# The spare-item loop of an attention + MoE + SwiGLU kernel: one chunk of both matrices per turn of an inner loop

## The chip, the cores and the metric

One core of a Trainium2 chip runs the whole program in one launch. The metric is the device time of one execution in microseconds (us). Engines are named as in the profile: PE is TensorE (its weight loads are PEld, its sequencer PEq or PEldq), DVE is VectorE, ACT is ScalarE, POOL is GpSimd, SP is SyncE, which here only issues transfers.

## What is computed

Three stages in a row, on 1536 tokens of 512 values, all in float32:

```python
x = attention(q, k, v)            # 8 heads, a band of 16 keys each way + 24 block summaries
logits = x @ w_gate + modality_bias[modality_id]
e_idx = argmax(logits); gate_w = softmax(logits)[e_idx]
for e in range(8):                # each token goes to one expert
    h = relu(x[e_idx == e] @ w1[e])            # 512 -> 1024
    y[e_idx == e] = gate_w * (h @ w2[e])       # 1024 -> 512
out = (silu(y @ w_g) * (y @ w_v)) @ w_o        # 512 -> 1536 -> 512
```

## The kernel before

The program has a written-out order on every engine. The attention comes first, the routing is computed beside its end, then the experts follow (the MoE), and then the dense SwiGLU stage.

**The experts.** Every product of two float32 matrices is made of three PE products of a high and a low part (`mm3`, L805 to L808). The tokens of an expert are gathered into items. Five items stand in the program as straight code (`KIND = "TQQSP"`): the largest expert takes an item of three blocks of 128 tokens, then come two of four blocks, one of a single block and one of two blocks. Each item multiplies by `w1` in four chunks of 256 hidden columns (`hidden`) and by `w2` (`project`). Its weight chunks, 512 KB each, are fetched by SP (L802), so the five items make 5 x 8 = 40 fetches; ACT and DVE split each into a high and a low part (L787, L788).

**The spare loop.** How many items are really needed is known only on the chip. Line 1342 loads the number of items beyond the five, `n_over`, into a register of every engine. At L1363 each engine compares it with zero. If it is positive, the loop at L1364 makes one spare item of two blocks per turn: gather, `split_x` (8 transposes on PE, L767), four `hidden` of 24 products each, and four chunks of `project`, 24 products each. If it is zero, a short else part raises the semaphores by what the body would have added, and jumps over the body (L1363 in the profile as well). The body lies in line in each engine's program, between that jump and the SwiGLU stage.

**Just before the branch** the last item ends: PE's last products of L806 to L808 into `ps_V`, ACT's `yh` (L1357) and DVE's `yl` (L1358), the high and low part of the MoE's output.

**Just behind it** the SwiGLU stage begins (`gv`): PE makes 12 products into `ps_T` for the gate (`gh`, `gl`), 12 for the value (`vh`, `vl`), and so on; ACT loads the table for Silu and makes `sg` (L1403), DVE `hv` (L1405). `ps_T` has three PSUM banks. From there to the end PE works through six blocks of 256 inner columns, while DVE decodes the next block's weights, fetched by SP (L1209). The last block adds each result to `acc` (L1422), and POOL scatters the rows to the output (L1427).

Of the kernel before, what the change touches and what calls it, by code (L numbers as in the profile page):

```python
# [7 lines left out]
F32 = mybir.dt.float32  # L8
F32R = mybir.dt.float32r
# [3 lines left out]
ALU = mybir.AluOpType  # L13
# [6 lines left out]
def sparse_attention_moe_swiglu_kernel(  # L20
# [18 lines left out]
    nc = tc.nc  # L39
    B, H, S, D = q.shape  # L40
# [25 lines left out]
    IT = 256  # L66
# [13 lines left out]
    KD = DM // 128  # L80
    NC1 = FF // 256
# [9 lines left out]
    def bank(tag):  # L91
        t = ps.tile([128, 512], F32, tag=tag, bufs=BANKS[tag], name="ps_" + tag)
        return t
# [81 lines left out]
    ident = const.tile([128, 128], F32, name="ident")  # L175
# [56 lines left out]
    for n in range(6):  # L232
        t = b_p[n // 3].tile([W, NG, H, D + 1], F32, tag=f"ve{n}", name=f"ve{n}")
# [497 lines left out]
    pl = {}  # L731
# [12 lines left out]
    def gather(pool, *cols, rows=NTOK):  # L744
        xs = []
        for ia in cols:
            t = pool.tile([128, DM + 1], F32, tag="xs", bufs=4, name="xs")
            nc.gpsimd.indirect_dma_start(out=t, out_offset=None, in_=x_d[0:rows, :],
                                         in_offset=bass.IndirectOffsetOnAxis(ap=ia, axis=0))
            xs.append(t)  # L750
        return xs

    def scale_x(xs):
        for t in xs:
            nc.vector.tensor_scalar(out=t[:, 0:DM], in0=t[:, 0:DM], scalar1=t[:, DM:DM + 1], scalar2=None, op0=ALU.mult)
# [27 lines left out]
    def split_w(pool, src, eng, tags=("wh", "wl")):  # L783
        a, b = src.shape[1], src.shape[2]
        wh = pool.tile([128, a, b], F32R, tag=tags[0], name="wh")
        wl = pool.tile([128, a, b], F32R, tag=tags[1], name="wl")
        nc.scalar.activation(out=wh, in_=src, func=ACTF.Copy)  # L787
        eng.tensor_tensor(out=wl, in0=src, in1=wh.bitcast(F32), op=ALU.subtract)  # L788
        return wh, wl

    def load_w(pool, e, which, c):
        r = pool.tile([128, KD, 256], F32, tag="raw", name="raw")
        if which == "w1":
            src = w1[bass.ds(e, 1), :, 256 * c:256 * c + 256]
        elif which == "rows":

            src = w2[bass.ds(e, 1), 256 * c:256 * c + 256, :].rearrange("e (k p) f -> p (e k) f", p=128)
            nc.sync.dma_start(out=r.rearrange("p (k a) f -> p k (a f)", k=2), in_=src)
            return r
        else:  # L800
            src = w2[bass.ds(e, 1), 512 * (c % 2):512 * (c % 2) + 512, 256 * (c // 2):256 * (c // 2) + 256]
        nc.sync.dma_start(out=r, in_=src.rearrange("e (k p) f -> p (e k) f", p=128))  # L802
        return r

    def mm3(out_, ah, al, bh, bl, start, stop):  # L805
        nc.tensor.matmul(out=out_, lhsT=ah, rhs=bh, start=start, stop=False)  # L806
        nc.tensor.matmul(out=out_, lhsT=ah, rhs=bl, start=False, stop=False)  # L807
        nc.tensor.matmul(out=out_, lhsT=al, rhs=bh, start=False, stop=stop)  # L808

    def hidden(c, x, w, later=None, tags="TT", between=None):  # L810
        n = x[0].shape[2]
        hh = pl["h"].tile([128, 2, n], F32R, tag="hh", name="hh")
        hl = pl["h"].tile([128, 2, n], F32R, tag="hl", name="hl")
        per = 512 // n
        for f0 in range(0, 2, per):
            if f0 and between is not None:
                between()
            p = bank(tags[f0])[:, 0:per * n].rearrange("p (f c) -> p f c", f=per)
            for f in range(f0, f0 + per):
                sl = slice(128 * f, 128 * f + 128)  # L820
                for kk in range(KD):
                    mm3(p[:, f - f0, :], w[0][:, kk, sl], w[1][:, kk, sl], x[0][:, kk, :], x[1][:, kk, :], kk == 0,
                        kk == KD - 1)
            fs = slice(f0, f0 + per)
            nc.scalar.activation(out=hh[:, fs], in_=p, func=ACTF.Relu)

            def low(p=p, fs=fs):
                nc.vector.scalar_tensor_tensor(out=hl[:, fs], in0=p, scalar=0.0, in1=hh[:, fs].bitcast(F32),  # L828
                                               op0=ALU.max, op1=ALU.subtract)

            if later is None:
                low()
            else:
                later.append(low)
        return hh, hl


    def project(c, hs, w, yp, cols=(0, 1), between=None):
        for k in range(4):
            if k == 2 and between is not None:  # L840
                between()
            kk = 4 * (c % 2) + k
            h = hs[kk // 2]
            for dd in cols:
                sl = slice(128 * dd, 128 * dd + 128)
                own = len(yp) == 1 and len(cols) == 2
                y = yp[0][:, dd] if own else yp[dd][:, 0]
                mm3(y, w[0][:, k, sl], w[1][:, k, sl], h[0][:, kk % 2, :], h[1][:, kk % 2, :],
                    kk == 0 and (dd == 0 or not own), kk == 2 * NC1 - 1 and (dd == 1 or not own))

    def y_banks(n, tag):
        if n == 256:
            return [bank(tag).rearrange("p (d c) -> p d c", d=2)]
        return [bank(tag)[:, 0:n].rearrange("p (d c) -> p d c", d=1) for _ in range(2)]

    def store_y(dp, yp, a, v_):
        for i, y in enumerate(yp):
            nd = 2 // len(yp)
            ds = slice(2 * dp + nd * i, 2 * dp + nd * i + nd)
            nc.scalar.activation(out=yh[:, ds, a], in_=y, func=ACTF.Copy)  # L860
            nc.vector.tensor_tensor(out=yl[:, ds, v_], in0=y, in1=yh[:, ds, v_].bitcast(F32), op=ALU.subtract)
# [141 lines left out]
    for st, names in steps.items():  # L1003
        for nm in names.split():
            b, t, j = (int(c) for c in nm[1:])
# [94 lines left out]
    hs, later = [], []  # L1100
# [19 lines left out]
    yp = [y_banks(CT, "S")]  # L1120
# [146 lines left out]
    def column(j):  # L1267
        return [eng.value_load(tab[0:1, 1, j:j + 1], min_val=0, max_val=before(j)) for eng in (nc.scalar, nc.vector)]
# [6 lines left out]
    hs = []  # L1275
# [5 lines left out]
    sa, sd = column(1)  # L1281
    for c in range(NC1):
        if c % 2 == 0:
            yp = y_banks(512, "T" if c else "S")
# [17 lines left out]
    hs, h1, hb = [], [], []  # L1302
# [19 lines left out]
    sa, sd = column(2)  # L1322
    for c in range(NC1):
        if c % 2 == 0:
            yp = y_banks(512, "T" if c else "S")
# [10 lines left out]
    hs = []  # L1336
# [9 lines left out]
    sa, sd = column(NS - 1)  # L1346
    ws = {}
    for tag, d0, cols in (("S", 0, (0, 1)), ("S", 2, (0,)), ("V", 3, (1,))):
        nd = len(cols)
        yp = bank(tag).rearrange("p (d c) -> p d c", d=2)[:, 0:nd]  # L1350
# [9 lines left out]
    bg_step(100)  # L1360


    with tc.If(n_over > 0, preferred_fallthrough_block=False):  # L1363
        with tc.For_i(0, n_over, 1) as it:  # L1364
            ii = pl["xg"].tile([128, 2], I32, tag="ii", name="ii")
            nc.vector.tensor_copy(out=ii, in_=idx[:, bass.ds(it * NB + NB * NS, 2)])
            e = nc.sync.value_load(tab[0:1, 0, bass.ds(it + NS, 1)], min_val=0, max_val=E - 1)
            xo = gather(pl["xg"], ii[:, 0:1], ii[:, 1:2])
            scale_x(xo)
            xo = split_x(pl["xg"], xo)  # L1370
            hs = [hidden(c, xo, split_w(pl["wc"], load_w(pl["raw"], e, "w1", c), nc.vector)) for c in range(NC1)]
            sa = nc.scalar.value_load(tab[0:1, 1, bass.ds(it + NS, 1)], min_val=0, max_val=NTOK)
            sd = nc.vector.value_load(tab[0:1, 1, bass.ds(it + NS, 1)], min_val=0, max_val=NTOK)
            for c in range(NC1):
                if c % 2 == 0:
                    yp = y_banks(IT, "S")
                project(c, hs, split_w(pl["wc"], load_w(pl["raw"], e, "w2", c), nc.vector), yp)
                if c % 2:
                    store_y(c // 2, yp, bass.ds(sa, IT), bass.ds(sd, IT))
    moe.close()  # L1380


# [94 lines left out]
```

## Time and profile before

| | |
|---|---|
| time, median of 3 runs | 596.92 us (596.2 to 598.31) |
| the profiled execution's own time | 597.52 us |
| its span, first to last instruction | 595.8 us |
| PE busy | 566.1 us, 95% of the span |
| DVE, ACT, POOL busy | 65%, 35%, 12% |
| mean granted clock of PE | 0.985 of full |

What lies around the span is 597.52 - 595.8 = 1.7 us. A time in a row is in us from the span's start. A name that ends in q (PEldq, SPq) is that engine's sequencer: branches, semaphore waits and the issuing of transfers stand there and are not counted as busy. `[4.31 <-issue]` behind a row says that the engine had been idle for 4.31 us before it, and that the profile shows no engine that it waited for. q8 and q14 of kind "instruction" are the queues on which the engines' own programs are fetched.

### The profile page before, as it was taken

Reading aid. Unit: us, or ns where it says so; the run is one execution under the profiler, and the core shown is the slowest. Engines: PE = TensorE matmul, PEld = TensorE weight load, DVE = VectorE, ACT = ScalarE, POOL = GpSimd, SP = SyncE. Lnnn points to the kernel's source line nnn. Section 1 sums busy time; section 2 is a strip of 40 time slices with the busy share of each in tenths; the row PEclk is TensorE's granted clock in tenths of the full one; section 3 lists DMA queues with packets and bytes.
Section 4 is the critical chain, followed back from the end, with each engine's and each line's share of the span. In section 5 each row is a group of like instructions: output and inputs, shape, how many; then the busy total and the mean of one; then the engine's idle time right before and its main releaser. Section 6 shows DMA issues by size and latency. Waiting matters only on the chain.

```text
span 595.8 us, 8863 instructions
## 1 busy us (share of the span) xinstructions
PE 566.1 (95%) x3372; PEld 474.3 (80%) x3372; DVE 384.8 (65%) x760; ACT 211.2 (35%) x370; POOL 69.8 (12%) x196
## 2 busy tenths in 40 slices
PE   7979997998996999999799999999999999999996
PEld 6769985998785888899588888888888888888884
DVE  6667796677978468674257568558738837863323
ACT  6766944443332354363223332212212212211110
POOL 6573012040202000100000000000000000000025
PEclk9999999999997999999899999999999999999999
DMA  9999238445634455561022222112203212200013
GB/s 249 212 261 202 79 91 261 136 146 167 202 127 124 125 174 172 163 202 47 3 72 70 72 80 93 40 36 84 93 0 107 71 36 70 72 0 1 0 72 141
DMA packets 76429, 64.84 MB, mean 109 GB/s; under 512 B 24340, under 2 KB 70432, under 8 KB 76192
## 3 DMA queue, kind: packets, MB, share of 16 engines
q1 hardware_dynamic: 74304, 57.41, 34.8%
q0 software_dynamic: 2080, 6.82, 3.4%
q8 instruction: 28, 0.46, 0.3%
q14 instruction: 17, 0.14, 0.1%
HBM read 57.88 MB, written 6.35 MB: 108 GB/s over the span
## 4 chain that ended last, share of the span: by engine, by line
PE 47%; issue 3%; POOL 2%; DVE 0%; POOLq 0%
PE ps_T L806 11%; PE ps_T L808 11%; PE ps_T L807 11%; PE ps_S L806 2%; PE ps_S L808 2%; PE ps_S L807 2%; POOL out_dram L1427 2%; PE ps_P L806 1%; PE ps_V L806 1%; PE ps_V L808 1%; PE ps_P L807 1%; PE ps_V L807 1%; PE ps_P L808 1%; DVE acc L1422 0%; POOL between L1425 0%
## 5 line engine op out<-in xcount | busy, mean ns | idle before, releaser
L1405 DVE TENSOR_TENSOR hv<-sg,ps_T 128x512 f32<-128x512 f32 x36 | 24.7, 687 | 74.4 <-PE ps_T L808 74.4
L806 PE MATMUL ps_T<-yh,gh 128*128 128x512 f32 x144 | 57.6, 400 | 4.3 <-issue 4.3
L788 DVE TENSOR_TENSOR wl<-raw,wh 128x1024 fp32r<-128x1024 f32 x40 | 48.9, 1223 | 17.8 <-ACT wh L787 17.2
L1407 ACT ACTIVATE fh<-hv 128x512 fp32r<-128x512 f32 x36 | 22.8, 632 | 103.9 <-DVE hv L1405 103.9
L808 PE MATMUL ps_T<-yh,gl 128*128 128x512 f32 x144 | 57.6, 400 | 0.0
L807 PE MATMUL ps_T<-yl,gh 128*128 128x512 f32 x144 | 57.4, 399 | 0.0
L808 PE MATMUL ps_T<-yh,vl 128*128 128x512 f32 x144 | 56.9, 395 | 0.0
L806 PE MATMUL ps_T<-yh,vh 128*128 128x512 f32 x144 | 56.9, 395 | 0.0
L807 PE MATMUL ps_T<-yl,vh 128*128 128x512 f32 x144 | 56.9, 395 | 0.0
L1427 POOL DMA_INDIRECT out_dram<-acc,tk x12 | 11.7, 977 | 325.4 <-DVE acc L1422 323.7
L787 ACT ACTIVATE wh<-raw 128x1024 fp32r<-128x1024 f32 x40 | 41.9, 1055 | 21.9 <-PE ps_S L807 8.8
L806 PE MATMUL ps_T<-xh,wh 128*128 128x512 f32 (+2 forms) x124 | 44.7, 361 | 0.3 <-DVE hl L828 0.3
L807 PE MATMUL ps_T<-xl,wh 128*128 128x512 f32 (+2 forms) x124 | 43.9, 354 | 0.0
L1403 ACT ACTIVATE sg<-ps_T 128x512 f32<-128x512 f32 x36 | 21.3, 591 | 63.7 <-PE ps_T L808 63.7
L808 PE MATMUL ps_T<-xh,wl 128*128 128x512 f32 (+2 forms) x124 | 43.8, 353 | 0.0
L1409 DVE TENSOR_TENSOR fl<-hv,fh 128x512 fp32r<-128x512 f32 x36 | 24.9, 693 | 25.1 <-ACT fh L1407 25.1
L806 PEld LDWEIGHTS ps_T<-yh,gh 128*128 128x128 f32 x144 | 27.4, 190 | 11.1 <-issue 4.5
L807 PEld LDWEIGHTS ps_T<-yl,gh 128*128 128x128 f32 x144 | 27.4, 190 | 6.7
L808 PEld LDWEIGHTS ps_T<-yh,gl 128*128 128x128 f32 x144 | 27.3, 190 | 6.7
L807 PEld LDWEIGHTS ps_T<-yl,vh 128*128 128x128 f32 x144 | 27.0, 188 | 6.6
L806 PEld LDWEIGHTS ps_T<-yh,vh 128*128 128x128 f32 x144 | 27.0, 188 | 6.6
L808 PEld LDWEIGHTS ps_T<-yh,vl 128*128 128x128 f32 x144 | 27.0, 188 | 6.6
(309 smaller groups left out, 1305.5 us busy)
## 6 DMA issues: line engine op xcount, KB each, us to landing
raw<-in_moe_w_dram SPq DMA_DIRECT2D x40, 512.0 KB, 3.4
r<-in_moe_w_gate_dram SPq DMA_DIRECT2D x12, 512.0 KB, 3.7
r<-in_moe_w_val_dram SPq DMA_DIRECT2D x12, 512.0 KB, 3.7
r<-in_moe_w_out_dram SPq DMA_DIRECT2D x12, 512.0 KB, 3.3
ve<-in_v_dram SPq DMA_DIRECT2D x20, 192.0 KB, 5.5
ld<-in_k_dram SPq DMA_DIRECT2D x12, 256.0 KB, 3.4
ld<-in_q_dram SPq DMA_DIRECT2D x12, 256.0 KB, 5.5
x_d<-x SPq DMA_DIRECT2D x12, 256.0 KB, 4.4
```

The costliest lines, as they stand in the source:

```text
L787: nc.scalar.activation(out=wh, in_=src, func=ACTF.Copy)
L788: eng.tensor_tensor(out=wl, in0=src, in1=wh.bitcast(F32), op=ALU.subtract)
L806: nc.tensor.matmul(out=out_, lhsT=ah, rhs=bh, start=start, stop=False)
L807: nc.tensor.matmul(out=out_, lhsT=ah, rhs=bl, start=False, stop=False)
L808: nc.tensor.matmul(out=out_, lhsT=al, rhs=bh, start=False, stop=stop)
L1403: nc.scalar.activation(out=sg, in_=gp_, func=ACTF.Silu)
L1405: nc.vector.tensor_tensor(out=hv, in0=sg, in1=vp_, op=ALU.mult)
L1407: nc.scalar.activation(out=hh, in_=hv, func=ACTF.Copy)
L1409: nc.vector.tensor_tensor(out=hl, in0=hv, in1=hh.bitcast(F32), op=ALU.subtract)
L1427: st = nc.gpsimd.indirect_dma_start(out=out, in_=acc[n], in_offset=None, out_offset=bass.IndirectOffsetOnAxis(ap=tk[:, 0:1], axis=0))
```

## The change

The body of the spare loop is written anew; nothing else is touched. Its four `hidden` and four `project` chunks, one behind the other, become an inner loop over the chunks, `tc.For_i(0, NC1, 1)`. One turn fetches a chunk of 256 columns of `w1` and the 256 rows of `w2` that go with it, makes the hidden chunk and at once its share of all four output chunks. The sums lie in two `ps_S` banks over all turns. Since a product inside a loop can't be the first or the last of its sum at a time known beforehand, each bank is opened and closed by a product of zeros (`nothing`); DVE makes the zeros once per item.

```diff
     with tc.If(n_over > 0, preferred_fallthrough_block=False):
         with tc.For_i(0, n_over, 1) as it:
...
             xo = split_x(pl["xg"], xo)
-            hs = [hidden(c, xo, split_w(pl["wc"], load_w(pl["raw"], e, "w1", c), nc.vector)) for c in range(NC1)]
+            zero = pl["h"].tile([128, 2, IT], F32R, tag="hh", name="zero")
+            nc.vector.tensor_scalar(out=zero.rearrange("p f (a c) -> p (f a) c", a=2),
+                                    in0=ident.unsqueeze(1).to_broadcast([128, 4, 128]), scalar1=0.0, scalar2=None,
+                                    op0=ALU.mult)
+
+            def nothing(y, start, stop):
+                nc.tensor.matmul(out=y.rearrange("p d c -> p (d c)"), lhsT=zero[:, 0, 0:128],
+                                 rhs=zero.rearrange("p f c -> p (f c)"), start=start, stop=stop)
+
+            yp = [bank("S").rearrange("p (d c) -> p d c", d=2) for _ in range(2)]
+            for y in yp:
+                nothing(y, True, False)
+            with tc.For_i(0, NC1, 1) as c:
+                w = pl["raw"].tile([128, KD, 256], F32, tag="raw", name="raw")
+                nc.sync.dma_start(out=w, in_=w1[bass.ds(e, 1), :, bass.ds(c * 256, 256)]
+                                  .rearrange("e (k p) f -> p (e k) f", p=128))
+                hh, hl = hidden(0, xo, split_w(pl["wc"], w, nc.vector))
+                w = pl["raw"].tile([128, KD, 256], F32, tag="raw", name="raw")
+                nc.sync.dma_start(out=w.rearrange("p (k a) f -> p k (a f)", k=2),
+                                  in_=w2[bass.ds(e, 1), bass.ds(c * 256, 256), :]
+                                  .rearrange("e (k p) f -> p (e k) f", p=128))
+                wh, wl = (t.rearrange("p (k a) f -> p k (a f)", k=2) for t in split_w(pl["wc"], w, nc.vector))
+                for dd in range(KD):
+                    sl = slice(128 * dd, 128 * dd + 128)
+                    for k in range(2):
+                        mm3(yp[dd // 2][:, dd % 2], wh[:, k, sl], wl[:, k, sl], hh[:, k, :], hl[:, k, :], False, False)
             sa = nc.scalar.value_load(tab[0:1, 1, bass.ds(it + NS, 1)], min_val=0, max_val=NTOK)
             sd = nc.vector.value_load(tab[0:1, 1, bass.ds(it + NS, 1)], min_val=0, max_val=NTOK)
-            for c in range(NC1):
-                if c % 2 == 0:
-                    yp = y_banks(IT, "S")
-                project(c, hs, split_w(pl["wc"], load_w(pl["raw"], e, "w2", c), nc.vector), yp)
-                if c % 2:
-                    store_y(c // 2, yp, bass.ds(sa, IT), bass.ds(sd, IT))
+            for dp in range(2):
+                nothing(yp[dp], False, True)
+                store_y(dp, [yp[dp]], bass.ds(sa, IT), bass.ds(sd, IT))
```

A blank line ahead of the branch moves every line number behind it by one, and the new text those behind the loop by 23 (L1403 becomes L1426).

PE's program before, from the last product ahead of the branch (the first row) to the first product of the SwiGLU stage (the last row); the line of dots stands for the other products of the spare body, 191 of them:

```order
L808 MATMUL ps_V<-hh,wl 128x256
L1363 COMPARE_AND_BRANCH
L1363 UNCONDITIONAL_BRANCH
L1364 COMPARE_AND_BRANCH
L1364 UNCONDITIONAL_BRANCH x2
L1472 BRANCH_PREFETCH_HINT
L767 MATMUL ps_V<-ident,xs 128x128 x4
L767 MATMUL ps_P<-ident,xs 128x128 x4
L806 MATMUL ps_T<-xh,wh 128x256
...
L1364 REGISTER_ALU
L1364 COMPARE_AND_BRANCH
L1364 UNCONDITIONAL_BRANCH
```

The second row (L1363) is the test, the third the jump of the else part; its target is the row behind the last one shown, the SwiGLU stage's first product. Between them lie 8 transposes and 192 products.

The same place of PE's program now, the dots standing for the other 47 products of the inner loop's one turn:

```order
L1364 COMPARE_AND_BRANCH
L1364 UNCONDITIONAL_BRANCH
L1365 COMPARE_AND_BRANCH
L767 MATMUL ps_V<-ident,xs 128x128 x4
L767 MATMUL ps_P<-ident,xs 128x128 x4
L1378 MATMUL ps_S<-zero 128x512 x2
L1384 COMPARE_AND_BRANCH
L806 MATMUL ps_T<-xh,wh 128x256
...
L1384 REGISTER_ALU
L1378 MATMUL ps_S<-zero 128x512 x2
L1365 REGISTER_ALU
```

The jump is now the second row, L1364. Between it and the SwiGLU stage lie 8 transposes, 48 products and 4 products of zeros, 60 in place of 200, and the branches and semaphore instructions of one more loop. Each product is two PE instructions, the weight load and the product itself; with the control instructions counted, 436 PE instructions of the built program lie between jump and target before, and 183 now. Ahead of the branch and behind the loop every engine's operations stand in the same order as before.

## Rows read from the trace of the kernel before

**Rows 1.** The page: busy time by engine, PE's program queue, the expert weights' fetches.

```profile
PE 566.1 (95%) x3372; PEld 474.3 (80%) x3372; DVE 384.8 (65%) x760; ACT 211.2 (35%) x370; POOL 69.8 (12%) x196
...
q8 instruction: 28, 0.46, 0.3%
...
raw<-in_moe_w_dram SPq DMA_DIRECT2D x40, 512.0 KB, 3.4
```

**Rows 2.** Waits by engine over the whole span: who waited for whom, us in total, times, longest.

```profile
PE ps_T L806 <- issue: 4.3, 1, 4.3
...
PE ps_V L767 <- issue: 2.0, 1, 2.0
```

**Rows 3.** PE by time around the branch: start, us, operation, tiles, idle before it.

```profile
282.44 0.28 PE L808 MATMUL ps_V<-hh,wl 128*128 128x256 f32 x1
287.03 0.47 PE L806 MATMUL ps_T<-yh,gh 128*128 128x512 f32 x1 [4.31 <-issue]
...
291.21 0.39 PE L808 MATMUL ps_T<-yh,gl 128*128 128x512 f32 x1
...
294.01 0.39 PE L808 MATMUL ps_T<-yh,vl 128*128 128x512 f32 x1
```

**Rows 4.** Line 1363, the branch, by engine: durations ns min/median/max, first and last start.

```profile
L1363 SPq COMPARE_BRANCH  x2: 38/48/57, 269.4 to 272.6; - x2
...
L1363 PEldq COMPARE_BRANCH  x2: 87/1860/3633, 280.4 to 282.9; - x2
...
L1363 DVEq COMPARE_BRANCH  x2: 51/53/55, 283.2 to 283.9; - x2
```

**Rows 5.** The first instructions behind the branch on PE, DVE and SP (lines 806, 1405, 1209).

```profile
L806 PEldq EVENT_SEMAPHORE  x4: 51/51/51, 286.6 to 286.9; - x4
L1405 DVEq EVENT_SEMAPHORE  x1: 10020/10020/10020, 284.4 to 284.4; - x1
L1209 SPq EVENT_SEMAPHORE  x1: 17/17/17, 273.1 to 273.1; - x1
```

**Rows 6.** Instruction queue q8 in the windows 262:282, 282.5:285.5, 286.5:290 and 300:580.

```profile
q8 instruction: 1, 0.02, 0.3%
q8 instruction: 1, 0.02, 2.6%
q8 instruction: 1, 0.02, 1.8%
q8 instruction: 10, 0.16, 0.3%
```

**Rows 7.** ACT and DVE by time around the branch.

```profile
283.18 0.43 DVE L1358 TENSOR_TENSOR yl<-ps_V,yh 128x256 f32 x1 [2.45 <-ACTq L1363]
283.74 1.28 ACT L1403 ACT_TABLE_LOAD   x1 [0.60 <-DVEq L1363]
...
294.51 0.69 DVE L1405 TENSOR_TENSOR hv<-sg,ps_T 128x512 f32<-128x512 f32 x1 [10.91 <-PE ps_T L808]
```

**Rows 8.** PE by time: two shorter idle stretches earlier in the program.

```profile
9.79 1.12 PE L687 MATMUL ps_S<-kb,qz 128*128 128x120 f32 x8 [1.56 <-ACT qz L645]
141.37 0.66 PE L767 MATMUL ps_P<-ident,xs 128*128 128x128 f32 x4 [1.14 <-DVE xl L770]
```

**Rows 9.** Stretches: us; busy PE, PEld, DVE, ACT, POOL; granted PE clock, DMA share, GB/s.

```profile
9.79:13.79 4.00, 4.00 (x34) 3.91 (x35) 2.84 (x7) 2.52 (x6) 1.71 (x7) 1.00 1.22 290
101.45:105.45 4.00, 3.24 (x15) 2.26 (x16) 3.02 (x9) 1.65 (x4) 0.00 (x0) 0.72 0.82 196
141.37:145.37 4.00, 4.00 (x25) 4.00 (x26) 2.46 (x3) 1.55 (x2) 0.00 (x0) 1.00 0.38 122
287.00:291.00 4.00, 3.97 (x11) 3.13 (x12) 0.00 (x0) 0.00 (x0) 0.00 (x0) 0.57 0.02 4
291.00:570.00 279.00, 279.00 (x1201) 225.10 (x1200) 173.65 (x300) 64.44 (x110) 3.29 (x7) 1.00 0.18 55
```

## Prediction

> **What bounds the kernel now.** Begin with whether the changed code runs. The page counts 40 fetches of expert weights [rows 1], which is exactly the 5 x 8 of the five items that stand as straight code. So `n_over` is 0 with these inputs, and the spare loop's body is passed over once by every engine. Its own speed, better or worse, is worth nothing here: the new inner loop, the zeros, the different weight fetches all cost 0 because they don't execute. What executes is the jump over the body. Everything ahead of the branch and behind the loop is the same work in the same order, so the change can act only through the jump: where it goes, how far, and what the engines do meanwhile.
>
> Next, read the waits. PE is busy for 95% of the span [rows 1], and its idle time is in a handful of places. One of the largest, 4.3 us at L806, is put down to "issue": PE waited for no engine [rows 2]. By time it lies exactly at the branch: the last product of the MoE starts at 282.44 and lasts 0.28, the first of the SwiGLU stage starts at 287.03 [rows 3]. Behind it PE is busy without a break from 291 to 570 [rows 9], so whatever is taken from this gap moves the whole rest of the program forward.
>
> What fills the gap is seen in the branch's own rows. On SP and DVE each of the two branch instructions takes 38 to 57 ns. On PE the first takes 87 ns and the second, the jump over the body at 282.9, takes 3633 ns [rows 4]. It ends at 286.5, the semaphore waits of the next product begin at 286.6 [rows 5], and 0.4 us later PE works. The instruction queue says why: PE's program comes in 28 packets of 0.46 MB together, 16 KB each [rows 1]. PE executes 3372 products with as many weight loads; with the 436 instructions that are passed over and some hundred control instructions that makes some 7,250, and 28 packets of some 256 instructions. One such packet comes between 262 and 282, then one in the three microseconds in which PE stands at the jump, and at once another [rows 6]. In straight code there are 10 in 280 us, and PE never stops for them [rows 6, 9]. So the jump goes to code that isn't there yet, and PE waits for it to be fetched.
>
> **What the change moves.** *Term 1, the jump.* It passed over 436 PE instructions, 1.7 packets; now it passes over 183, 0.7 of a packet. A target less than one packet ahead lies, wherever the packet borders are, in the packet being executed or in the next one, and the next one had come before 282 [rows 6]. So I expect no fetch at the jump. Its record should then be like PE's other one, 0.09 us, from 282.9 to 283.0. What follows such a jump is seen on two other engines: on SP the next instruction begins at 273.1, 0.5 us after the jump at 272.6, on DVE at 284.4, 0.5 after 283.9 [rows 4, 5]. I take 0.5 for PE too, so its waits begin at 283.5. The first product waited in four semaphore instructions, 0.4 us; now the same product has three, 0.3. It starts at 283.8 in place of 287.03 [rows 3]: **3.2 us** gained. Bounds: with 0.1 instead of 0.5, as on PE after the fetch (286.5 to 286.6), it would start at 283.4, but the second product reads `yl`, which DVE finishes at 283.18 + 0.43 = 283.6 [rows 7]; so no more than 3.5 can be had. At the other end the jump still fetches, and the gain is 0.
>
> *Term 2, the clock.* [...] From 287.03 to 291.21 it starts eleven more products, 4.18 us; the twelve steps from 291.21 to 294.01 take 2.80, 0.233 each, and eleven of those are 2.57 [rows 3]. So the low clock costs 1.6 us. Another idle stretch, 2.0 us ahead of 101.45, is followed by 0.72 as well; those of 1.56 us (ahead of 9.79) and of 1.14 us (ahead of 141.37) are followed by the full clock [rows 2, 8, 9]. The stretch left here is 283.8 - 282.7 = 1.1 us, like the shortest of these, so I take the whole **1.6 us**; the bounds are 0 and 1.6.
>
> *What costs nothing.* The jumps of ACT, DVE, POOL and SP pass over 15 to 30 instructions more (SP two fewer), since a loop's control is repeated on each engine. Were one of them to meet missing code and wait 3.6 us as PE does, DVE has 10.9 us of idle time ahead of `hv`. ACT has its table load at 283.74, 1.28 long [rows 7]; 3.6 later it would end at 288.6, and `sg` could follow. PE goes on for three groups of 12 products, 2.8 us each [rows 3], in the three `ps_T` banks before it needs the first again, at 283.8 + 8.4 = 292.2. SP's next transfer waits for a weight tile that DVE decodes only after its first `hv` and `fl`. If that cover were gone, one such wait would cost at most 3.6.
>
> *The sum.* 3.2 + 1.6 = 4.8 us off the profiled execution's own 597.52 (span 595.8 and 1.7 around it): 592.7. That execution stands 0.6 above the median of the runs, 596.92. From the median the forecast is **592.1 us**, 0.8% less. Differences under 0.3%, 1.8 us, can't be told from none by a measurement of this kernel.
>
> **The rivals.** *A. The stall isn't about distance.* PE runs deep queues of products, and a taken jump might restart them with a fetch however near its target is. PE makes no other taken jump in this trace, so nothing here excludes it; against it is that the jumps of DVE and SP, which have their own program queue, cost 0.5 us. Then the kernel stays at 596.9. For the row itself: one packet comes per 256 instructions, the next only at the jump [rows 6], so PE's program is not held far ahead. [...]
>
> *B. The clock still falls.* The remaining 1.1 us of idleness comes with a few slower starts around it, and that is enough for the low level. Then only term 1 is had: 596.92 - 3.2 = 593.7. For it: there is no case between 1.56 and 2.0 us, and the fall after 2.0 shows that the border is near. Against it: two shorter stretches without one [rows 8, 9].
>
> *C. Slower: the next packet isn't asked for.* In before, the fetch at the jump was followed at once by the next packet's [rows 6]. A jump into a packet that is already there might ask for nothing; PE would then come to that packet's end, some 200 instructions or 25 us behind the jump, without the code that follows. The price is what it was at the jump: 4.3 us of idleness less the 0.2 of a product, plus 1.6 for the clock, 5.7 together. Once, that gives 592.1 + 5.7 = 597.8, no change; from the second packet missed it decides, 603.5, and the loss goes on with each of the 10 behind. Against it: in straight code PE enters packet after packet that is already there, and the next is asked for each time [rows 6].
>
> **How the numbers follow.** The forecast gets 0.74, B 0.13, A with every way in which the jump still fetches 0.09, C 0.04 with its single miss counted as no change. Term 1's bounds move the forecast by 0.3 down and, with a slower restart of the queues, by as much up; the runs before spread by 0.7 below and 1.4 above their median. So the forecast with its noise reaches from 591.0 to 593.4, and B, with its own noise, to 594.6. From 591.0 to 594.6 the range leaves out A and C, 0.13. Faster by over 0.3% (under 595.1): 0.74 + 0.13 = 0.87, and 0.01 for a part of A in which the wait is only shortened, 0.88. Within 0.3%: the rest of A and C's single miss, 0.09. Slower by over 0.3%: 0.03.
>
> **What would show it.** In the profile of the changed kernel, PE's second branch record should be near 0.1 us and not 3.6; a q8 packet may come then, for the code behind the one jumped into, but PE doesn't wait for it; the idle time before that product should be 1.0 to 1.3 us, with `yl` or "issue" as what ended it; the first twelve products should follow each other by 0.233 us at a granted clock of 1.00; ACT's first `sg` should stand near 286.7, and everything behind should keep its distances. A branch record still at 3.6 us with a packet beside it shows A; a short record with products 0.43 apart shows B; a second idle stretch some 25 us behind the branch shows C. The forecast is wrong outright if `n_over` isn't 0, which 40 weight fetches exclude, or if an idle stretch of PE appears that isn't here now.

## The result, and the profile after

The changed kernel takes 592.02 us (median of 4 runs, 588.82 to 593.37), the kernel before 597.26 (4 runs, 596.2 to 598.31): a ratio of 0.9902, 95% interval 0.9878 to 0.9926. The forecast was 592.1.

The spare loop still isn't executed: 40 weight fetches, as in [rows 1]. The page of the changed kernel:

```profile
PE 566.7 (96%) x3372; PEld 476.0 (80%) x3372; DVE 386.0 (65%) x760; ACT 211.3 (36%) x370; POOL 69.4 (12%) x196
...
q8 instruction: 27, 0.44, 0.3%
...
raw<-in_moe_w_dram SPq DMA_DIRECT2D x40, 512.0 KB, 3.4
```

The branch's own rows (line 1364 now), and the first semaphore waits behind it (line 806); the columns are those of [rows 4, 5]:

```profile
L1364 SPq COMPARE_BRANCH  x2: 37/47/57, 270.2 to 270.5; - x2
L1364 PEldq COMPARE_BRANCH  x2: 95/200/304, 281.2 to 283.7; - x2
...
L1364 DVEq COMPARE_BRANCH  x2: 51/53/55, 284.0 to 284.6; - x2
...
L806 PEldq EVENT_SEMAPHORE  x3: 51/51/51, 284.1 to 284.3; - x3
```

PE's jump takes 304 ns in place of 3633. By time, the answer to [rows 3]:

```profile
283.24 0.28 PE L808 MATMUL ps_V<-hh,wl 128*128 128x256 f32 x1
284.39 0.47 PE L806 MATMUL ps_T<-yh,gh 128*128 128x512 f32 x1 [0.87 <-ACTq L1364]
...
287.03 0.39 PE L808 MATMUL ps_T<-yh,gl 128*128 128x512 f32 x1
```

The idle stretch is 0.87 us in place of 4.31, and the first eleven steps behind it take 287.03 - 284.39 = 2.64 us in place of 4.18. The granted clock no longer falls there (1.00, where it was 0.57), and PE is busy to 570 as it was [rows 9]; the stretches of the changed kernel, with the columns of [rows 9]:

```profile
284.00:288.00 4.00, 3.61 (x16) 3.00 (x17) 0.40 (x1) 1.82 (x2) 0.00 (x0) 1.00 0.02 6
288.00:570.00 282.00, 282.00 (x1214) 227.50 (x1213) 174.21 (x301) 64.51 (x111) 4.29 (x8) 1.00 0.17 57
```

So the idle time gave 3.44 us and the clock 1.54, together 4.98. The two profiled executions differ by 597.52 - 593.37 = 4.15 only, because the last MoE product starts at 283.24 here and at 282.44 there. That part of the program is the same in both; in the ten profiles of this study the start lies between 281.3 and 284.2. A measure free of it is the time from that start to the end of the span: 595.8 - 282.44 = 313.36 before, 591.6 - 283.24 = 308.36 now, 5.00 less. The experiments are read by it.

### The profile page after: what moved, and what is told of

The parts are those of the page before. It is cut to its first block, busy times and chain, and to the rows that moved or that the text cites. A ratio compares the mean times of both kernels' runs of the same rounds, so it can differ in the third digit from the quotient of the medians.

```text
span 591.6 us, 8853 instructions
## 1 busy us (share of the span) xinstructions
PE 566.7 (96%) x3372; PEld 476.0 (80%) x3372; DVE 386.0 (65%) x760; ACT 211.3 (36%) x370; POOL 69.4 (12%) x196
## 4 chain that ended last, share of the span: by engine, by line
PE 47%; issue 2%; POOL 2%; POOLq 0%; DVE 0%
PE ps_T L806 11%; PE ps_T L808 11%; PE ps_T L807 11%; PE ps_S L806 3%; PE ps_S L808 2%; PE ps_S L807 2%; POOL out_dram L1450 1%; PE ps_P L806 1%; PE ps_V L806 1%; PE ps_P L807 1%; PE ps_V L808 1%; PE ps_V L807 1%; PE ps_P L808 1%; POOLq L1495 0%; POOL between L1448 0%
## 5 line engine op out<-in xcount | busy, mean ns | idle before, releaser
L806 PE MATMUL ps_T<-yh,gh 128*128 128x512 f32 x144 | 57.0, 396 | 0.9 <-ACTq L1364 0.9
L806 PE MATMUL ps_T<-yh,vh 128*128 128x512 f32 x144 | 56.9, 395 | 0.0
L806 PE MATMUL ps_T<-xh,wh 128*128 128x512 f32 (+2 forms) x124 | 45.1, 364 | 0.3 <-DVE hl L828 0.3
L1426 ACT ACTIVATE sg<-ps_T 128x512 f32<-128x512 f32 x36 | 21.3, 592 | 58.3 <-PE ps_T L808 58.3
L806 PEld LDWEIGHTS ps_T<-yh,gh 128*128 128x128 f32 x144 | 27.0, 188 | 7.5 <-ACTq L1364 1.0
L806 PEld LDWEIGHTS ps_T<-yh,vh 128*128 128x128 f32 x144 | 27.0, 188 | 6.6
```

The costliest lines, as they stand in the source:

```text
L1426: nc.scalar.activation(out=sg, in_=gp_, func=ACTF.Silu)
```

## The experiments

Three theories could give this result. **Packets**: PE's program comes in packets of some 256 instructions (an estimate: some 7,250 instructions in 28 packets [rows 1]); a jump waits when its target's packet hasn't been asked for, and only the packet behind the one being executed is asked for in advance. **Distance**: a jump further than some 256 instructions fetches, wherever it stands. **Rival A**, in the form that the short record leaves open: the stall belongs to the old body's kind (its straight code, its banks), and the inner loop removed it.

### The jump lengthened: 80, 104 and 116 more products of zeros

The changed kernel with n more products in the body that is passed over:

```diff
             for y in yp:
                 nothing(y, True, False)
+            for _ in range(n):
+                nothing(yp[0], False, False)
```

With 80:

> The changed kernel with 80 more products of zeros in the body that is passed over: the jump passes over 343 PE instructions, more than one packet of 256, and its target is instruction 4553 of PE's program. Packet theory (counted from 0 in packets of 256, the jump at 4209 stands in packet 16, the next packet holds 4352 to 4607 and had come): no fetch at the jump, PE's branch record near 0.3 us, idle stretch near 0.9 us, clock full behind it. Distance theory (any jump further than 256 instructions fetches): record near 3.6 us, idle stretch 4.3 us, low clock behind it, 5.0 us more. Rival A (the old body's other features, not its length): record near 0.3.

With 104:

> The same with 104 products: 391 instructions passed over, target 4601, seven ahead of the counted packet border at 4608. Packet theory: record near 0.3 us, idle stretch 0.9 us. Distance theory: 3.6 and 4.3 us.

With 116:

> The same with 116 products: 415 instructions passed over, target 4625, 17 behind the counted border. Packet theory: the target lies in packet 18, which isn't there; record near 3.6 us, a packet on q8 within it, idle stretch 4.3 us, low clock for some 3.5 us behind it, 5.0 us lost in all against the run with 104. Rival A: record near 0.3 us.

The times were 596.47, 596.05 and 599.68 us (one run each), the kernel before 597.6 beside them. The branch rows, first of the run with 80:

```profile
L1364 PEldq COMPARE_BRANCH  x2: 95/200/304, 280.2 to 282.7; - x2
```

With 104:

```profile
L1364 PEldq COMPARE_BRANCH  x2: 95/1742/3388, 279.2 to 281.7; - x2
```

With 116:

```profile
L1364 PEldq COMPARE_BRANCH  x2: 95/1772/3448, 282.2 to 284.7; - x2
```

343 instructions are passed over in 304 ns, 391 in 3388. Distance, with its bound at 256, is refuted by the first, and a stall that needs the old body by the other two, which have the new one. A distance with its bound between 343 and 391 would still fit all three; the shifted kernels below settle that. There is a border, but not where it was counted: the run with 104 was expected on the near side. The run with 80 shows where it lies, in DVE's last `yl` and PE by time with its weight loads, and in the instruction queue from 283 to 287:

```profile
282.94 0.43 DVE L1358 TENSOR_TENSOR yl<-ps_V,yh 128x256 f32 x1 [2.45 <-ACTq L1364]
283.40 0.19 PEld L806 LDWEIGHTS ps_T<-yh,gh 128*128 128x128 f32 x1 [1.12 <-ACTq L1364]
283.43 0.47 PE L806 MATMUL ps_T<-yh,gh 128*128 128x512 f32 x1 [0.94 <-ACTq L1364]
283.51 0.19 PEld L807 LDWEIGHTS ps_T<-yl,gh 128*128 128x128 f32 x1
...
286.21 0.55 PE L807 MATMUL ps_T<-yl,gh 128*128 128x512 f32 x1 [2.32 <-issue]
...
q8 instruction: 1, 0.02, 1.5%
```

The jump arrives at 4553 without a wait, PE goes through three semaphore waits, one product and one weight load, and then stands for 2.32 us between a weight load and its own product, although `yl` was written by then (282.94 + 0.43 = 283.37). A packet comes at 283.6, only behind the jump, which ended at 283.0. By the packet theory this is the packet that PE waits for, and PE has reached the end of one at instruction 4559 or so. The program's packets would thus begin some 49 instructions earlier than counted, with 256 to a packet at 4303, 4559, 4815. With that, 4601 and 4625 both lie one packet too far, and all three runs agree with the packet theory. The run with 80 also lost the clock (0.57 granted from 286 to 290), and so nearly the whole gain: 594.7 - 282.21 = 312.49 from the last MoE product to the end.

### The old body, the program shifted

> The kernel before, its spare body untouched (436 instructions passed over), with 45 one-column products (180 PE instructions) added at the very start of PE's program, whose results nobody reads. The jump now stands at 4389, in packet 17, its target at 4826, in packet 18. Packet theory: packet 18 has come when the jump is made; record near 0.3 us, idle stretch 0.9 us, no low clock behind the branch, though the body and the distance are those of before. Distance theory and rival A: record 3.6 us, idle stretch 4.3 us as in before.

```diff
     warm(11)
+    p_pad = bank("P")
+    for _ in range(45):
+        nc.tensor.matmul(out=p_pad[0:1, 0:1], lhsT=ident[:, 0:1], rhs=ident[:, 0:1], start=True, stop=True)
```

Measured: 596.3 us (one run), a record of 3428 ns, an idle stretch of 4.17 us. Taken alone it speaks for rival A. But it was laid out with the borders counted from 0; with the border that the run with 80 showed, its target, 4826, lies 11 instructions behind 4815, and the packet theory says a stall as well. So it tells nothing apart. The same with 30 products does:

> The run with 80 products stopped PE not at the jump but at instruction 4559 or 4560, so the packet borders lie some 49 instructions ahead of the counted ones: 4303, 4559, 4815. The shift by 180 had then put the target, 4826, behind the border at 4815. Now the kernel before, spare body untouched (436 passed over), with 30 one-column products (120 PE instructions) at the very start: jump at 4329, target 4766, in the packet 4559 to 4814. Packet theory: that packet had been asked for when PE entered 4303, so the record is near 0.3 us, the idle stretch 0.9 to 1.2, the clock stays full; if PE enters 4303 so shortly before the jump (26 instructions) that the packet is still on its way, the record is between 0.3 and 3.6. Rival A (the old body, or its length, makes the stall): record 3.4 to 3.6 us, idle stretch near 4.2.

It took 592.28 us (one run; before 597.32, median of 7). Its branch row, PE by time, and the instruction queue from 277 to 279, ahead of the jump:

```profile
L1366 PEldq COMPARE_BRANCH  x2: 91/202/314, 279.9 to 282.5; - x2
```

```profile
283.32 0.47 PE L809 MATMUL ps_T<-yh,gh 128*128 128x512 f32 x1 [1.15 <-DVEq L1366]
283.63 0.40 PE L810 MATMUL ps_T<-yl,gh 128*128 128x512 f32 x1
```

```profile
q8 instruction: 1, 0.02, 4.1%
```

This kernel has the spare body of before, word for word, and jumps as far, 436 instructions. The stall is gone, because by those borders jump and target now lie in neighbouring packets, and a packet, by the theory the target's, had come between 277 and 279, the jump following at 282.5: 314 ns, 1.15 us idle, and 590.6 - 281.89 = 308.71 to the end, the changed kernel's figure within 0.4. So neither the old body nor a distance of 436 instructions makes the stall by itself. With a border at 4559 the two shifted runs also bound the estimate of 256: by the packet theory 4329 and 4766 in neighbouring packets ask for at least 230 instructions to a packet, 4389 and 4826 in packets two apart for at most 267.

### The old body, shorter, without an inner loop

> The kernel before with three of the spare item's four hidden chunks left out (the first stands for all four; the body isn't executed): no inner loop, no products of zeros, but 292 PE instructions passed over in place of 436, target 4501, in the packet 4303 to 4558 and 58 instructions, some 7 us, ahead of its end. Packet theory: record 0.3 us, idle stretch 0.9, and the whole gain of the changed kernel: 4.3 - 0.9 + 1.6 = 5.0 us less than before, ratio 0.9916. Distance theory (more than 256) and every theory in which the inner loop itself brings the gain: no change, ratio 1.000, record 3.6.

```diff
-            hs = [hidden(c, xo, split_w(pl["wc"], load_w(pl["raw"], e, "w1", c), nc.vector)) for c in range(NC1)]
+            hs = [hidden(0, xo, split_w(pl["wc"], load_w(pl["raw"], e, "w1", 0), nc.vector))] * NC1
```

Measured: 593.47 us (4 runs) against 597.32 (7 runs), ratio 0.9927, interval 0.9897 to 0.9956. The point expected, 0.9916, lies in it, and 1.000 doesn't.

```profile
L1363 PEldq COMPARE_BRANCH  x2: 95/200/304, 282.0 to 284.5; - x2
```

PE by time in the same run:

```profile
285.21 0.47 PE L806 MATMUL ps_T<-yh,gh 128*128 128x512 f32 x1 [0.94 <-ACTq L1363]
285.51 0.39 PE L807 MATMUL ps_T<-yl,gh 128*128 128x512 f32 x1
```

592.4 - 283.99 = 308.41 to the end. A shorter body without the inner loop does what the inner loop did, with a target in the next packet, 58 instructions ahead of its end; 6 ahead of it, the run with 80 products stalled.

### The clock: idle without a fetch

> The changed kernel with DVE's last yl written nine times over (8 more of 0.43 us, the same values), so that PE waits at the same place as before for some 3.5 us more, but for DVE and not for its program. If the low clock follows idleness alone: the second product starts some 3.5 us later than in the changed kernel, the clock falls for some 3.5 us and costs 1.6 as in before, 5 us lost in all, near the time of before. If the low clock had to do with the fetch: full clock, 3.5 us lost.

```diff
-        nc.vector.tensor_tensor(out=yl[:, ds, bass.ds(sd, IT)], in0=yp, in1=yh[:, ds, bass.ds(sd, IT)].bitcast(F32),
-                                op=ALU.subtract)
+        for _ in range(9 if tag == "V" else 1):
+            nc.vector.tensor_tensor(out=yl[:, ds, bass.ds(sd, IT)], in0=yp, in1=yh[:, ds, bass.ds(sd, IT)].bitcast(F32),
+                                    op=ALU.subtract)
```

It took 598.8 us (one run). PE by time, then the stretches:

```profile
284.64 0.47 PE L806 MATMUL ps_T<-yh,gh 128*128 128x512 f32 x1 [0.87 <-ACTq L1365]
288.44 0.51 PE L807 MATMUL ps_T<-yl,gh 128*128 128x512 f32 x1 [3.33 <-DVEq L1365]
...
289.68 0.63 PE L808 MATMUL ps_T<-yh,gl 128*128 128x512 f32 x1
...
292.24 0.59 PE L808 MATMUL ps_T<-yh,gl 128*128 128x512 f32 x1
```

```profile
284.50:288.40 3.90, 0.47 (x1) 0.19 (x1) 3.56 (x9) 0.00 (x0) 0.00 (x0) 1.00 0.02 4
288.40:292.40 4.00, 3.96 (x11) 3.14 (x12) 0.00 (x0) 1.28 (x1) 0.00 (x0) 0.61 0.01 2
```

The jump is as short as in the changed kernel (304 ns), PE waits for DVE instead, and the clock falls to 0.61 over four microseconds, as it fell to 0.57 in before [rows 9]. From the last MoE product to the end it is 597.0 - 283.49 = 313.51, 5.15 more than in the changed kernel: some 3.5 of waiting and 1.6 of the clock. So the clock's part of the gain comes from the idleness being short, whatever ended it: behind the idle stretches of 0.87, 0.94 and 1.15 us in these runs the clock granted over the next four microseconds was 1.00, behind those of 2.32 to 4.31 us 0.50 to 0.62.

### Without the branch

> The kernel before without the test, the jump and the spare body (nothing of them is executed on these inputs except the test and the jump). It bounds what is left at this place: the first SwiGLU product then waits for yh and yl alone. yl ends 0.93 us after the last MoE product's end in the changed kernel's profile, where the second product waits for it; so the idle stretch should shrink from 0.87 to about 0.6 and the second product gain 0 to 0.2 us. Theory: ratio to before 0.991, like the changed kernel's, within 0.3 us of it. Rival: the branch costs more than the record shows (semaphores on ACT, DVE and SP), 1 us or more below the changed kernel.

Lines 1363 to 1379 are left out, and with them the spare item that other inputs may need. Measured: 592.91 us (4 runs) against 597.32 (7 runs), ratio 0.9934, interval 0.9908 to 0.996. By time, PE and DVE:

```profile
283.08 0.28 PE L808 MATMUL ps_V<-hh,wl 128*128 128x256 f32 x1
283.20 0.40 PE L806 MATMUL ps_T<-yh,gh 128*128 128x512 f32 x1
283.43 0.40 PE L807 MATMUL ps_T<-yl,gh 128*128 128x512 f32 x1
...
283.81 0.43 DVE L1358 TENSOR_TENSOR yl<-ps_V,yh 128x256 f32 x1 [2.45 <-ACT yh L1357]
```

The expectation of a stretch of 0.6 us was wrong: there is none. PE's first products don't wait for the last `yh` and `yl`: the second one, which reads `yl`, starts at 283.43, and DVE begins the last part of `yl` at 283.81. From the last product to the end it is 590.3 - 283.08 = 307.22, 1.14 less than in the changed kernel. That is what the branch still costs, 0.2%, and the runs can't tell it (592.91 and 592.02).

Where the 1.1 us go is seen in the changed kernel's rows at the branch:

```profile
L1364 PEldq EVENT_SEMAPHORE  x1: 51/51/51, 283.6 to 283.6; - x1
L1364 ACTq EVENT_SEMAPHORE  x2: 17/17/17, 284.0 to 284.1; - x2
```

Most of it is PE's own sequence. The else part raises PE's semaphore at 283.6, behind PE's last product (283.24 + 0.28), the jump follows at 283.7 with its 0.304 us, and the three semaphore instructions of L806 from 284.1 to 284.3; then the product starts. The profile puts these 0.87 us down to ACT, but none of the three is held: they take 51 ns each, ACT's first semaphore had come at 284.0, and where PE is held in such an instruction the record is longer, 114 ns for one of the four in the kernel shifted by 30:

```profile
L809 PEldq EVENT_SEMAPHORE  x4: 51/51/114, 282.8 to 283.2; - x4
```

That the else part can also join PE to another engine's last work is seen with the late `yl`: there the second product waits until DVE's semaphore of the else part, 3.33 us, for a `yl` that it doesn't wait for when the branch is gone.

### All of them together

| kernel | jump at, target | packets between | record, ns | idle, us | last MoE product to end, us |
|---|---|---|---|---|---|
| before | 4209, 4646 | two on | 3633 | 4.31 | 313.36 |
| changed | 4209, 4393 | next | 304 | 0.87 | 308.36 |
| 80 more | 4209, 4553 | next, 6 ahead of its end | 304 | 0.94 + 2.32 | 312.49 |
| 104 more | 4209, 4601 | two on | 3388 | 3.96 | 313.04 |
| 116 more | 4209, 4625 | two on | 3448 | 4.09 | 313.68 |
| shifted, 45 | 4389, 4826 | two on | 3428 | 4.17 | 313.11 |
| shifted, 30 | 4329, 4766 | next | 314 | 1.15 | 308.71 |
| fewer hidden | 4209, 4501 | next | 304 | 0.94 | 308.41 |
| late `yl` | 4209, 4393 | next | 304 | 0.87 + 3.33 | 313.51 |
| no branch | none | | | 0 | 307.22 |

The positions are counted in the built program of PE; the packets are those with the borders 4303, 4559 and 4815, as read from the run with 80 products. No version here is measurably faster than the changed kernel.

## Why the prediction was right

**The bound and the mechanism** were read rightly: a body that isn't executed, an idle stretch that only the jump explains, and a branch record of 3633 ns beside a packet on q8 [rows 4, 6]. That the target's packet decides is shown by the shifted kernel, which has the old body and the old distance and no stall, and by the runs with 80 and 104 products, 48 instructions apart, of which one waits at the jump (3388 ns) and the other doesn't (304).

**Term 1** was 3.2 us and measured 3.44, inside its bounds. The restart was taken as 0.5 us behind a record of 0.09, from SP and DVE; on PE it stands inside the record, 0.304, and the next instruction follows 0.06 later. So the record was taken 0.2 too short and the restart 0.4 too long, and the two partly cancel; the idle stretch of 0.87 lies below the 1.0 to 1.3 that was named. Three semaphore waits instead of four came as the order showed.

**Term 2** was 1.6 us and measured 1.54. The granted clock was 0.57 from 287 to 291 in before [rows 9] and 1.00 from 284 to 288 in the changed kernel. The late `yl` shows by itself that idleness of this length costs it.

**The sum** was 4.8 us; the trace gives 4.98, and the medians 5.24 with an interval from 0.7 to 1.2% of the time, 4.4 to 7.3 us. That the forecast of 592.1 meets the median of 592.02 to 0.1 us is luck: the four runs of the changed kernel spread over some 4.5 us, and two of them, 590.89 and 588.82, lie below the range. The range's upper end also doesn't follow from the parts that are given for it: B's 593.7 with the 1.4 us that the runs spread upward makes 595.1, not 594.6. The measured median lies inside by either.

**A step that was too simple**: "a target less than one packet ahead" was said to be safe wherever the borders lie. In the changed kernel it was safe from a fetch at the jump (304 ns), but the run with 80 products shows the missing condition: a packet, by the theory the one behind the target's, comes only 0.6 us behind the jump's end there and 0.8 in the changed kernel, so a target close to its packet's end stalls a few instructions later, 2.32 us there. The changed kernel has some 165 instructions from its target to that end, by an estimate 19 us at 0.233 us per product. It wasn't known then that the borders were 49 instructions off the count; 183 passed over could have met one, so this part of the forecast came true by luck.

**The rivals.** A, a fetch at a taken jump however near its target, falls by the changed kernel's own record of 304 ns, though PE does run ahead: in before its test stands at 280.4, 2.0 us before the start of the last product, which precedes it in PE's order [rows 3, 4]. That the old body's kind makes the stall falls by the kernel shifted by 30, which has that body. B's way, a clock that still falls, didn't happen at 0.87 us of idleness (1.00 granted). C didn't happen either: in the changed kernel a packet comes at 284.8, 0.8 us behind the jump's end, in the window from 284.4 to 288.

```profile
q8 instruction: 1, 0.02, 1.9%
```

Every run agrees with packets of 16 KB [rows 1], no wait at a jump into the next one (a record of 0.30 to 0.31 us), and 3.4 to 3.6 us at a jump into the one after. PE's program isn't held far ahead: the jump over 391 instructions already waits, 3388 ns.

## What to carry to other kernels

Code that is passed over can cost time: 436 instructions in the kernel before cost 5.0 us more than 183 in the changed one. Where a branch record is long on one engine and the instruction queue moves beside it, count that engine's instructions between the jump and its target. Keep the body short, or place it so that the target falls into the packet behind the jump's own and well ahead of that packet's end (58 instructions were enough here, 6 were not). Then look what the idleness did to the clock: here it was a third of the price, 1.54 us of 4.98.

## What was unexpected

- PE's packets begin some 49 instructions earlier than a count of the built program says, as read from the run with 80 products. Two of the first four experiments were laid out too close to the counted border, and one of them, read by the counted border, would have spoken for the wrong theory.
- A jump that meets its code takes 0.30 us on PE against 0.04 to 0.05 on SP and DVE; the test ahead of it takes 0.09 there.
- Even with a short jump, the branch costs about 1.1 us at this place, most of it in PE's own semaphore instructions and the jump, one behind the other; without it, PE passes on with no idle time at all.
